# Activation transposes of a fused attention and feed-forward backward: from TensorE to DMA transposes

## Chip, cores and metric

One core of one Trainium2 chip. The metric is the device time of one execution in microseconds (us), median of the runs. The kernel is called "before", the changed one "after".

## The reference, cut to what matters

A pre-norm block with linear attention (32 heads of 20), then a SwiGLU feed-forward, and the gradients of everything. S = 2048 tokens, D = 640, F = 1728, all bf16.

```python
def _fwd_reference(A_x, A_wqkv, A_wo, B_x, B_w_gate, B_w_up, B_w_down):
    ...                               # _A_ref: linear attention, _B_ref: SwiGLU
    x = A_x
    h = x + _A_ref(_layernorm(x, axis=-1), A_wqkv, A_wo)
    h2 = h + _B_ref(_layernorm(h, axis=-1), B_w_gate, B_w_up, B_w_down)
    return h2

def reference(A_x, A_wqkv, A_wo, B_w_gate, B_w_up, B_w_down, B_x, grad_out):
    ...
    _out, _vjp = jax.vjp(_f, A_x, A_wqkv, A_wo, B_w_gate, B_w_up, B_w_down)
    return (_out, *_vjp(grad_out))    # output and six gradients
```

Forward products sum over features, weight gradients over tokens. In this kernel's matmuls the index that is summed over lies on the partitions (the 128 rows of a tile), so many activations are needed in both layouts: token-major ("tm", tokens on the partitions) and feature-major ("fm").

## The kernel before: the parts concerned

A transpose of a 128x128 block is a TensorE instruction into PSUM, up to eight of them side by side, and a copy out by VectorE or ScalarE in turn:

```python
def transpose_into(dst_fn, src_fn, nblk, rows_in, ps_pool, tag="tr", cols_in=P, group=8, eng=None):
    ...
    while b < nblk:
        nb = min(group, nblk - b)
        pt = ps_pool.tile([P, 8 * P], BF16, name="pt_" + tag, tag=tag)
        for j in range(nb):
            nc.tensor.transpose(out=pt[:cols_in, j * rows_in:(j + 1) * rows_in], in_=src_fn(b + j),
                                identity=ident[:rows_in, :rows_in])
        evac_copy(dst_fn(b, nb), pt[:cols_in, :nb * rows_in], eng)
        b += nb
```

The feed-forward loop takes two rows of 128 features ("a group") per pass: projections into feature-major rows, stores of the rows to DRAM for later stages, transposes of the rows into token-major strips, then weight gradients from the strips.

```python
strips = pb2.enter_context(tc.tile_pool(name="strips", bufs=1))
...
for grp in groups:                                   # 7 groups of 2 rows
    ...
    for i in grp:
        ...                                          # pg, pu, pdm matmuls; mT_row, dgT_row, duT_row
        nc.gpsimd.dma_start(out=scr_mT_v[:, i, :], in_=mT_row[:, :])
        nc.gpsimd.dma_start(out=scr_dgT_v[:, i, :], in_=dgT_row[:, :])
        nc.gpsimd.dma_start(out=scr_duT_v[:, i, :], in_=duT_row[:, :])
        for (row, strip) in ((mT_row, m_strip), (dgT_row, dg_strip), (duT_row, du_strip)):
            transpose_into(...)                      # 16 blocks each
        coff += fs
    ...                                              # acc: m_strip x dh2; accw: hn x dg_strip, du_strip
```

Later, in the backward attention, six tensors are transposed one after another, two of them after a reload from DRAM:

```python
pq_tm = ...; fm_to_tm(pq_tm, pqTr, D, psTD)
dnum_tm = ...; fm_to_tm(dnum_tm, dnumT, D, psTD)
...                                                  # dKV matmuls
nc.sync.dma_start(out=pk_tmr[:], in_=scr_pk_tm_v)
pkT = ...; tm_to_fm(pkT, pk_tmr, D, psTD)
nc.sync.dma_start(out=v_tmr[:], in_=scr_v_tm_v)
vT = ...; tm_to_fm(vT, v_tmr, D, psTD)
...                                                  # ps_dv and ps_dk matmuls need all of pkT and vT
```

## Time and profile before

| | before |
|---|---|
| median time | 1115.46 us (2 runs, 1115.44 to 1115.48) |
| TensorE busy | 1056.7 us, 95% of the span |
| transposes concerned | 1632 blocks of 128x128, about 93 us of TensorE issue |
| DMA | 134 MB, 120 GB/s over the span |
| feed-forward loop | 60.2 us a group, seven groups |

Read the busy shares first, to see which engine is full; then the chain that ended last, to see whether that engine also sets the end; then single groups. The prediction shows these lines.

### The profile page before, as it was taken

The page shows a single profiled execution, that of the slowest core. Times are in us where ns is not written, and L with a number is a line of the kernel's source. Part 1 is how long each engine was busy: PE and PEld are TensorE (multiplying, and loading weights), DVE is VectorE, ACT ScalarE, POOL GpSimd, SP SyncE. Part 2 cuts the span into 40 slices and gives each one's busy share as a digit, 9 for nine tenths or more (in the row PEclk, how much of TensorE's full clock was granted, in tenths as well). Part 3 has the DMA queues.
Part 4 walks back from the last instruction along what each step waited for, and adds up shares of the span by engine and source line. Part 5 has one row for each costly group of instructions (what it writes and reads, how often), then busy time and mean ns, then how long its engine had stood idle before and what let it go on. Part 6 is the DMA issues. An engine that isn't in the chain of part 4 may idle for free.

```text
span 1114.9 us, 20384 instructions
## 1 busy us (share of the span) xinstructions
PE 1056.7 (95%) x8337; PEld 714.7 (64%) x8337; DVE 571.8 (51%) x1441; ACT 483.0 (43%) x951; POOL 133.4 (12%) x224
## 2 busy tenths in 40 slices
PE   5899998999999999999996999599989999899998
PEld 2477665575847576666756777377767467577775
DVE  8766676727273545545361232234343985477321
ACT  5755587526262535345351010122233686744231
POOL 2100000120202111111312013000000000011110
PEclk9899899999999999999999999799999999999999
DMA  8244364312222222212045954955440039411110
GB/s 318 75 138 150 159 247 146 125 61 86 92 82 96 78 103 78 98 41 107 31 159 182 219 136 139 298 119 122 100 153 31 1 123 351 181 39 43 42 36 30
DMA packets 134669, 134.24 MB, mean 120 GB/s; under 512 B 92384, under 2 KB 115680, under 8 KB 134320
## 3 DMA queue, kind: packets, MB, share of 16 engines
q0 software_dynamic: 20208, 77.58, 18.8%
q1 hardware_dynamic: 85440, 48.03, 15.4%
q10 hardware_dynamic: 28928, 7.34, 3.4%
q8 instruction: 65, 1.06, 0.4%
q14 instruction: 28, 0.23, 0.1%
HBM read 71.50 MB, written 61.42 MB: 119 GB/s over the span
## 4 chain that ended last, share of the span: by engine, by line
PE 69%; DMA 6%; DVE 6%; issue 1%; ACT 1%; POOL 0%; POOLq 0%; DVEq 0%; ACTq 0%; SPq 0%
PE accw L561 10%; PE acch L663 10%; PE acc_dxn L837 6%; PE accf L621 6%; PE acc_dwqkv L856 6%; PE pu L498 4%; PE pg L494 4%; PE acc L552 4%; PE pt_trs L127 4%; PE pt_tr L127 3%; PE pdm L502 3%; DMA dgcols<-scr_dgT 3%; PE acc_dwo L697 2%; PE ps_do L721 2%; DVE dm L519 1%
## 5 line engine op out<-in xcount | busy, mean ns | idle before, releaser
L561 PEld LDWEIGHTS <-hn_tm 128*128 128x128 bf16 x1120 | 107.1, 98 | 16.0 <-issue 4.8
L494 PE MATMUL pg<-hnT,wg_blk 128*128 128x512 bf16 (+1 forms) x280 | 76.2, 384 | 3.3 <-DMA wg_blk<-in_B_w_gate_dram 3.3
L663 PE MATMUL acch<-wgT,dgcols 128*128 128x320 bf16 x448 | 67.9, 304 | 12.0 <-DMA dgcols<-scr_dgT 11.5
L498 PE MATMUL pu<-hnT,wu_blk 128*128 128x512 bf16 (+1 forms) x280 | 74.7, 379 | 0.0
L89 DVE CAST dw_sb<-accw 128x256 bf16<-128x256 f32 (+1 forms) x35 | 14.5, 415 | 111.7 <-PE accw L561 86.8
L502 PE MATMUL pdm<-dh2T,wdT 128*128 128x512 bf16 (+1 forms) x280 | 69.6, 379 | 1.1 <-ACT dm L511 1.0
L552 PE MATMUL acc<-dh_tm,m_strip 128*128 128x320 bf16 (+1 forms) x448 | 69.3, 299 | 0.0
L621 PE MATMUL accf<-wd_big,mcols 128*128 128x320 bf16 x448 | 64.8, 306 | 3.6 <-DMA mcols<-scr_mT 3.6
L663 PE MATMUL acch<-wuT,ducols 128*128 128x320 bf16 x448 | 66.4, 300 | 0.0
L856 PE MATMUL acc_dwqkv<-cur_tm,xn_tmr 128*128 128x320 bf16 x480 | 65.7, 299 | 0.0
L663 PEld LDWEIGHTS <-dgcols 128*128 128x128 bf16 x448 | 44.4, 99 | 30.4 <-DMA dgcols<-scr_dgT 11.8
L561 PE MATMUL accw<-dg_strip,hn_tm 128*128 128x256 bf16 (+1 forms) x560 | 60.5, 269 | 3.4 <-ACT dw_sb L91 2.9
L561 PE MATMUL accw<-du_strip,hn_tm 128*128 128x256 bf16 (+1 forms) x560 | 60.3, 269 | 0.7 <-DVE dw_sb L89 0.7
L856 PEld LDWEIGHTS <-xn_tmr 128*128 128x128 bf16 x480 | 46.9, 98 | 18.1
L621 PEld LDWEIGHTS <-mcols 128*128 128x128 bf16 x448 | 44.0, 100 | 22.1 <-DMA mcols<-scr_mT 3.7
L91 ACT CAST dw_sb<-accw 128x256 bf16<-128x256 f32 (+1 forms) x35 | 12.8, 364 | 103.8 <-PE accw L561 98.9
L214 ACT ACTIVATE lb_dy<-acch 128x320 bf16<-128x320 f32 x32 | 14.0, 436 | 97.6 <-PE acch L663 97.6
L663 PEld LDWEIGHTS <-ducols 128*128 128x128 bf16 x448 | 44.0, 98 | 17.3
L552 PEld LDWEIGHTS <-m_strip 128*128 128x128 bf16 (+1 forms) x448 | 41.8, 99 | 13.5 <-issue 0.3
L229 DVE SCALAR_TENSOR_TENSOR lb_t<-lb_dy,lb_nm,lb_t 128x640 bf16<-128x640 bf16 x32 | 28.2, 880 | 41.1 <-ACT lb_t L227 41.1
L502 PEld LDWEIGHTS <-wdT 128*128 128x128 bf16 (+1 forms) x280 | 27.0, 98 | 34.4 <-DVE wdT L89 3.1
L565 POOL DMA_DIRECT2D out_dram<-dw_sb x70 | 37.7, 539 | 79.5 <-DVE dw_sb L89 44.9
(264 smaller groups left out, 2068.2 us busy)
## 6 DMA issues: line engine op xcount, KB each, us to landing
scr_mT<-mT_row POOLq DMA_DIRECT2D x14, 512.0 KB, 2.9
scr_duT<-duT_row POOLq DMA_DIRECT2D x14, 512.0 KB, 3.7
scr_dgT<-dgT_row POOLq DMA_DIRECT2D x14, 512.0 KB, 2.9
ducols<-scr_duT ACTq DMA_DIRECT2D x16, 448.0 KB, 4.7
mcols<-scr_mT SPq DMA_DIRECT2D x16, 448.0 KB, 4.1
dgcols<-scr_dgT SPq DMA_DIRECT2D x16, 448.0 KB, 4.2
out_dram<-dw_sb POOLq DMA_DIRECT2D x60, 64.0 KB, 1.8
x_tm<-in_A_x_dram SPq DMA_DIRECT2D x4, 640.0 KB, 6.3
```

Of the source, the lines that this page charges most:

```text
L127: nc.tensor.transpose(out=pt[:cols_in, j * rows_in:(j + 1) * rows_in], in_=src, identity=ident[:rows_in, :rows_in])
L229: nc.vector.scalar_tensor_tensor(out=t2[:], in0=dy[:], scalar=nm[:, 0:1], in1=t1[:], op0=ALU.subtract, op1=ALU.subtract)
L494: nc.tensor.matmul(pg[:fs, :], lhsT=wg_blk[:, kt, coff:coff + fs], rhs=hnT[:, kt, cs], start=(kt == 0), stop=(kt == DT - 1))
L498: nc.tensor.matmul(pu[:fs, :], lhsT=wu_blk[:, kt, coff:coff + fs], rhs=hnT[:, kt, cs], start=(kt == 0), stop=(kt == DT - 1))
L502: nc.tensor.matmul(pdm[:fs, :], lhsT=wdT_i[:, kt, :], rhs=dh2T[:, kt, cs], start=(kt == 0), stop=(kt == DT - 1))
L552: nc.tensor.matmul(acc[:fs, :w], lhsT=m_strip[:, t, coff:coff + fs], rhs=dh2_tm[:, t, n0:n1], start=(t == 0), stop=(t == ST - 1))
L561: nc.tensor.matmul(acc[:, :gw], lhsT=hn_tm[:, t, dt_ * P:(dt_ + 1) * P], rhs=strip[:, t, :gw], start=(t == 0), stop=(t == ST - 1))
L565: nc.gpsimd.dma_start(out=o_ap[dt_ * P:(dt_ + 1) * P, gcol0:gcol0 + gw], in_=dw_sb[:, :gw])
L621: nc.tensor.matmul(acc[:, :w], lhsT=mcols[:, j, :], rhs=wd_nat[:, j, n0:n1], start=(j == 0), stop=(j == FT - 1))
L663: nc.tensor.matmul(acc[:, :w], lhsT=cols[:, j, :], rhs=wT[:, j, n0:n1], start=(k == 0), stop=(k == 2 * FT - 1))
L837: nc.tensor.matmul(acc[:, :w], lhsT=srcT[:, jj, t * P:(t + 1) * P], rhs=wqkvT[:, j, n0:n1], start=(k == 0), stop=(k == D3T - 1))
L856: nc.tensor.matmul(acc[:, :w], lhsT=xn_tmr[:, t, dt_ * P:(dt_ + 1) * P], rhs=cur_tm[:, t, n0:n1], start=(t == 0), stop=(t == ST - 1))
```

## The change

The intent is to free TensorE: it is the bound, and the DMA engines are mostly idle (busy share 0.38 over the span of before). All transposes of activations become DMA transposes on the SyncE queue, one per token tile ([128, 640], 5 blocks) or per feature tile ([128, 2048], 16 blocks). The small weight transposes stay on TensorE.

```diff
     def tm_to_fm(dstT, src_tm, W, ps_pool, eng=None, tag="tr"):
-        WT = W // P
-        for j in range(WT):
-            transpose_into(...)
+        for t in range(ST):
+            nc.sync.dma_start_transpose(out=dstT[:, :, t * P:(t + 1) * P], in_=src_tm[:, t, :])

     def fm_to_tm(dst_tm, srcT, W, ps_pool, eng=None, tag="tr"):
-        WT = W // P
-        for t in range(ST):
-            transpose_into(...)
+        for j in range(W // P):
+            nc.sync.dma_start_transpose(out=dst_tm[:, :, j * P:(j + 1) * P], in_=srcT[:, j, :])
 ...
     def tm_to_fm_tiles(dstT, src_tm, W, t0, nt, ps_pool, eng=None, tag="tr"):
-        ...
+        for t in range(t0, t0 + nt):
+            nc.sync.dma_start_transpose(out=dstT[:, :, t * P:(t + 1) * P], in_=src_tm[:, t, :])
 ...
                     for (row, strip) in ((mT_row, m_strip), (dgT_row, dg_strip), (duT_row, du_strip)):
-                        transpose_into(...)
+                        nc.sync.dma_start_transpose(out=strip[:, :, coff:coff + fs], in_=row[:fs, :])
```

More of the change, by code (lines that the diff above doesn't have):

```diff
@@ L132, in tm_to_fm @@
     def tm_to_fm(dstT, src_tm, W, ps_pool, eng=None, tag="tr"):
-        WT = W // P
-        for j in range(WT):
-            transpose_into(
-                dst_fn=lambda b0, nb, j=j: dstT[:, j, b0 * P:(b0 + nb) * P],
-                src_fn=lambda b, j=j: src_tm[:, b, j * P:(j + 1) * P],
-                nblk=ST, rows_in=P, ps_pool=ps_pool, eng=eng, tag=tag)
-    def fm_to_tm(dst_tm, srcT, W, ps_pool, eng=None, tag="tr"):
-        WT = W // P
-        for t in range(ST):
-            transpose_into(
-                dst_fn=lambda b0, nb, t=t: dst_tm[:, t, b0 * P:(b0 + nb) * P],
-                src_fn=lambda b, t=t: srcT[:, b, t * P:(t + 1) * P],
-                nblk=WT, rows_in=P, ps_pool=ps_pool, eng=eng, tag=tag)
+        for t in range(ST):
+            nc.sync.dma_start_transpose(out=dstT[:, :, t * P:(t + 1) * P], in_=src_tm[:, t, :])
+    def fm_to_tm(dst_tm, srcT, W, ps_pool, eng=None, tag="tr"):
+        for j in range(W // P):
+            nc.sync.dma_start_transpose(out=dst_tm[:, :, j * P:(j + 1) * P], in_=srcT[:, j, :])
     def layernorm_tiles(src_tm, dst_tm, mean, rstd, t0, nt, work, mode="bn"):
@@ L201, in tm_to_fm_tiles @@
     def tm_to_fm_tiles(dstT, src_tm, W, t0, nt, ps_pool, eng=None, tag="tr"):
-        WT = W // P
-        for j in range(WT):
-            transpose_into(
-                dst_fn=lambda b0, nb, j=j: dstT[:, j, (t0 + b0) * P:(t0 + b0 + nb) * P],
-                src_fn=lambda b, j=j: src_tm[:, t0 + b, j * P:(j + 1) * P],
-                nblk=nt, rows_in=P, ps_pool=ps_pool, eng=eng, tag=tag)
+        for t in range(t0, t0 + nt):
+            nc.sync.dma_start_transpose(out=dstT[:, :, t * P:(t + 1) * P], in_=src_tm[:, t, :])
     def ln_bwd_tile(acc_chunks, xhat_t, rstd_col, resid_t, dst_t, work):
@@ L527 @@
                     for (row, strip) in ((mT_row, m_strip), (dgT_row, dg_strip), (duT_row, du_strip)):
-                        transpose_into(
-                            dst_fn=lambda b0, nb, strip=strip, coff=coff, fs=fs: strip[:, b0:b0 + nb, coff:coff + fs],
-                            src_fn=lambda b, row=row, fs=fs: row[:fs, b * P:(b + 1) * P],
-                            nblk=ST, rows_in=fs, ps_pool=ps_tr, tag="trs", cols_in=P)
+                        nc.sync.dma_start_transpose(out=strip[:, :, coff:coff + fs], in_=row[:fs, :])
                     coff += fs
```

## The prediction

The sum was 0 (before the loop) + 10 (loop) + 8 (attention output) + 96 (four tensors) + 14 (last stage) = +128 us on 1115, rounded to 1240.

> **What bounds the kernel now.** I read the header of the page first, then the chain of work that ended last, then the groups of the transposes, then the windows by stage, and last the DMA queues, because the change moves work from TensorE to them.
>
> ```profile
> PE 1056.7 (95%) x8337; PEld 714.7 (64%) x8337; DVE 571.8 (51%) x1441; ACT 483.0 (43%) x951; POOL 133.4 (12%) x224
> PE 69%; DMA 6%; DVE 6%; issue 1%; ACT 1%; POOL 0%; POOLq 0%; DVEq 0%; ACTq 0%; SPq 0%
> ```
>
> TensorE is busy 95% of the span and carries 69% of the chain. There is hardly a stage where it waits: it is the bound nearly everywhere. So a microsecond of matmul issue taken away is worth about a microsecond, as long as nothing new makes TensorE wait. What the transposes cost it is in the groups by line and tile:
>
> ```profile
> L127 PE MATMUL pt_trs<-ident,mT_row 128*128 128x128 bf16 (+1 forms) x224 | 19.0, 217 | 1.2 <-DVE m_strip L89 0.3
> L127 PE MATMUL pt_trs<-ident,dgT_row 128*128 128x128 bf16 (+1 forms) x224 | 16.9, 217 | 0.2
> L127 PE MATMUL pt_trs<-ident,duT_row 128*128 128x128 bf16 (+1 forms) x224 | 16.6, 216 | 0.2
> ...
> L127 PE MATMUL pt_tr<-ident,dh_tm 128*128 128x128 bf16 x160 | 11.2, 219 | 0.5
> ```
>
> Busy time (the figure after the first bar) overlaps with neighbours; 217 ns is the latency of one, and they issue much faster. The chain in order of time has the pure rate in the backward attention stage:
>
> ```profile
> 910.04 8.63 PE pt_tr L127 x140
> ...
> 928.67 4.47 PE pt_tr L127 x80
> ...
> 933.57 4.64 PE pt_tr L127 x80
> ```
>
> 80 transposes take 4.5 to 4.6 us, 57 ns each, and there they stand on the chain with matmuls right before and behind. The windows say how much room the DMA engines have (columns: stretch, length, busy time of PE, PEld, DVE, ACT, POOL, granted clock, DMA share, GB/s):
>
> ```profile
> 305.00:366.00 61.00, 60.61 (x460) 39.97 (x459) 31.14 (x72) 26.52 (x46) 9.68 (x18) 1.00 0.24 86
> ...
> 908.00:930.00 22.00, 21.85 (x351) 21.21 (x350) 12.78 (x32) 11.84 (x20) 0.86 (x1) 1.00 0.94 335
> 930.00:961.00 31.00, 30.82 (x246) 17.73 (x244) 19.51 (x48) 29.98 (x48) 0.00 (x0) 1.00 0.52 189
> ```
>
> One group of the feed-forward loop (61 us, seven of them) leaves 76% of DMA free; the stage at 908 us, where four more tensors are to be transposed by DMA, has 94% busy already with reloads from DRAM.
>
> ```profile
> q1 hardware_dynamic: 85440, 48.03, 15.4%
> q10 hardware_dynamic: 28928, 7.34, 3.4%
> ```
>
> (Columns: packets, MB, share of 16 engines.) The second queue moves rows of 256 B: 3.4% of 16 engines' 1114.9 us is 606 us, over 28928 packets 21 ns each. 16 engines at 256 B in 21 ns are 195 GB/s; the first queue gives 32 ns a packet.
>
> [...]For DMA no row here shows a transpose. [...]All hangs on this rate.
>
> **The change part by part.** It removes 3x224 transposes of the feed-forward rows, and those of twelve tensors of 80 blocks each: 960. Together 1632 at 57 ns: 93 us of TensorE. In the loop there are 96 per group; the group's matmuls, at the rates of the chain, are 120 of 512 columns at 0.216 us (25.9), 64 of 320 at 0.136 (8.7) and 160 of 256 at 0.109 (17.5), 52.1 us against a period of 60.2. The ten small weight transposes stay (0.6 us), so 7.5 us per group, 52 us in seven, are what the loop can gain[...]. The evacuation copies go too: 41 us of ScalarE and 28 us of VectorE for the strips, but neither engine bounds this loop (26.5 and 31.1 of 61 us), so they are worth nothing.
>
> It adds 42 DMA transposes of [128, 2048] (16 blocks, 512 KB), 30 of the same size for the feature-to-token tensors, and 96 of [128, 640] (5 blocks, 160 KB): about 53 MB on top of 134 MB, all on the SyncE queue, which issues in order and also carries the weight loads and reloads.
>
> [...]To each I add 2 us from issue to landing, as the smallest stores of this trace need (1.8 to 2.1 us).
>
> Stage 1 (to 187 us): the transposes of the input follow LayerNorm[...]; those of the output gradient come off TensorE, 5 us; the second LayerNorm loses about what it gains. Sum 0.
>
> Loop: [...]the second row's three strips can only start when that row is done, about 3 us after its last matmul, behind the rest of the first row's. [...]TensorE has only 8.7 us of matmuls on the first strips before it needs the gradient strips; each strip tile has one buffer, so the next group's can't run ahead either. About 8 to 10 us of new wait per group against 7.5 gained: +1.5 times 7, +10.
>
> Backward attention: the attention output's transposes, pipelined by column block[...], +8 with the ones behind them. From 892 us, when buffers come free, four tensors in a row: [...]the kernel now starts the next matmuls at 938: +96. This is the biggest term: TensorE has only some 27 us of other work meanwhile.
>
> Last stage: [...]the first hidden behind 65 us of matmuls, the next two each behind 21.7[...], 8.4 us of TensorE transposes saved: +14.
>
> Sum 0+10+8+96+14 = +128: **1240 us**.
>
> **The rivals.** First, the transposes run near copy speed[...]. Then the loop gains 30 to 50 us, the four-tensor stage costs 0 to 30, the end gains 8: 1040 to 1085 us. For it: the 195 GB/s of the 256 B queue[...]. Against: [...]from 908 us the engines have 6% free. Second, [...]the loop[...] becomes DMA-bound (+25 times 7), the four-tensor stage +230, the rest some +150: about 1670 us[...]. Third, the rate is good but order costs: SyncE holds a load behind a transpose that waits for its source, and TensorE waits for a weight or a column block; some us per group, 20 to 60 us in all. It would make even the first rival a draw. Granted clock is no part of it: it is 0.9 to 1.0 now.
>
> **Range and chances.** [...]The draw is a narrow band of rates, one in seven. The slow side is open: 1240 with a range from 1070[...] to 1680[...]. Faster 0.17, within 2% 0.14, slower 0.69.
>
> **What would show it.** In the changed profile, the time from issue to landing and the spacing of the strip transposes give the rate[...]. TensorE's busy time should fall by some 90 to 120 us, to about 945, and its share to under 80%; its idle time should be put to DMA, largest before the matmuls that read the four backward tensors and before the gradient-strip matmuls of the loop. If the loop's period is under 56 us the rate is better than I think; if over 75 the loop is DMA-bound. If waits fall on weight loads instead, it is the order of the SyncE queue. I am wrong if the four tensors land within 60 us of each other, or if they are transposed earlier because buffers are free sooner than 892 us.

## The result, and the profile after

After: 1209.66 us median (1207.21 and 1212.12); the ratio to before is 1.0836, 95% interval 1.0773 to 1.0899. So it is slower. A ratio here is the mean time of one kernel's fast runs over that of the other's of the same rounds, so not quite the ratio of the medians.

The header and the chain of the page after:

```profile
PE 973.6 (81%) x6705; PEld 634.7 (53%) x6705; DVE 503.2 (42%) x1306; ACT 385.3 (32%) x813; POOL 134.2 (11%) x225
q1 hardware_dynamic: 296640, 100.74, 42.2%
PE 67%; DMA 18%; SPq 7%; DVE 3%; ACT 3%; issue 1%; POOLq 0%; DVEq 0%; ACTq 0%
```

TensorE did lose 83 us of busy time, as intended. But the chain has 18% of DMA instead of 6%, and a new member: 7% for SPq, the sequencer of SyncE, which before had none. The SyncE queue's packets went from 85440 to 296640.

Where the 90 us between the two profiled spans lie, from the first and last starts of a stage's matmuls in both traces:

| stretch (up to) | before | after | difference |
|---|---|---|---|
| first matmul of the feed-forward loop (pg) | 181.4 | 177.5 | -3.9 |
| first matmul of the next stage (accf): the loop | 431.4 | 467.8 | +36.4 |
| last matmul of acch | 207.4 | 208.3 | +0.9 |
| last matmul of ps_do | 68.6 | 78.6 | +10.0 |
| first matmul of acc_dxn: middle of the backward attention | 81.9 | 135.6 | +53.7 |
| first matmul of acc_dwqkv | 65.2 | 66.6 | +1.4 |
| end | 79.0 | 70.8 | -8.2 |

**The loop.** The chain of after in order of time (start, us, what), around the end of the first group:

```profile
208.32 14.52 DMA m_strip<-mT_row
...
222.88 6.87 PE acc L537 x32
229.76 2.29 PE accw L546 x21
```

The last projection of the group ends at 207 us. The transpose of the second row's first strip is issued at 208.3 and lands 14.5 us later. TensorE has the first row's matmuls on that strip until 211.3, and then stands for 11.6 us. The timeline of after says what was issued at that time (start, us; L512 to L514 are the row stores; other lines of VectorE, ScalarE and TensorE are left out):

```profile
206.82 4.51 PE L537 MATMUL acc<-dh_tm,m_strip 128*128 128x320 bf16 x32
207.64 0.53 POOL L512 DMA_DIRECT2D scr_mT<-mT_row  x1 [9.73 <-DVE mT_row L502]
207.75 0.47 SPq L458 DMA_DIRECT2D wu_blk<-in_B_w_up_dram  x1
208.32 7.42 SPq L516 DMA_TRANSPOSE m_strip<-mT_row  x1
208.36 0.53 POOL L514 DMA_DIRECT2D scr_duT<-duT_row  x1 [0.18 <-issue]
...
210.61 0.53 POOL L513 DMA_DIRECT2D scr_dgT<-dgT_row  x1 [1.72 <-DVE dgT_row L511]
```

In the same 3 us as the strip that TensorE waits for, three stores of the same rows (512 KB each, and nobody needs them for 400 us) start on the GpSimd queue; two weight loads of 320 KB (`wg_blk` and `wu_blk`) were issued just before. The windows of after (columns as in the prediction) for this wait, and for the rest of that group:

```profile
205.90:223.00 17.10, 5.54 (x39) 3.55 (x37) 4.04 (x10) 1.63 (x4) 2.14 (x4) 0.74 1.15 224
223.00:247.50 24.50, 24.50 (x198) 20.03 (x198) 2.61 (x6) 2.11 (x6) 5.39 (x10) 0.90 0.25 63
```

DMA engines full (share 1.15) and TensorE idle for most of it, then TensorE full and the DMA engines at a quarter. The granted clock is 0.74 in the wait and 0.90 after it, where the loop before had 1.00. The first 32 matmuls after the wait take 6.87 us in the chain. In the same trace, the 32 of the same shape just before the wait took 4.51. Over the seven groups, the groups by line of after put 71.7 us of idle TensorE on this one wait:

```profile
L537 PE MATMUL acc<-dh_tm,m_strip 128*128 128x320 bf16 (+1 forms) x448 | 75.1, 335 | 71.7 <-DMA m_strip<-mT_row 71.7
```

And the whole loop in the windows, before and after:

```profile
181.40:612.90 431.50, 420.18 (x3199) 276.04 (x3200) 217.09 (x505) 187.00 (x324) 72.79 (x130) 0.99 0.28 99
177.50:645.40 467.90, 384.22 (x2515) 245.94 (x2516) 191.25 (x459) 148.47 (x278) 73.54 (x131) 0.91 0.61 137
```

TensorE's idle time in the loop grew by 72 us (from 11 to 84), and its busy time fell by 36: that is the +36.

**The middle of the backward attention.** SyncE's timeline of after, and the load of v in that of before:

```profile
948.63 21.52 SPq L138 DMA_TRANSPOSE dnum_tm<-dnumT  x5
970.32 0.91 SPq L769 DMA_DIRECT2D pk_tmr<-scr_pk_tm  x1
982.05 21.02 SPq L134 DMA_TRANSPOSE pkT<-pk_tmr  x16
1003.18 0.51 SPq L773 DMA_DIRECT2D v_tmr<-scr_v_tm  x1
1013.50 21.04 SPq L134 DMA_TRANSPOSE vT<-v_tmr  x16
```

```profile
918.76 0.36 SPq L788 DMA_DIRECT2D v_tmr<-scr_v_tm  x1
```

A load, its 16 transposes, the next load, its 16 transposes: nothing overlaps. The load of v is issued only at 1003.2, when the sequencer is through with the transposes of pk; before, it was issued 10 us after the first transpose of this stage began (918.8 us against 908.6). And 16 transposes keep the sequencer busy for 21.0 us, one every 1.31 us. That is 160 KB in 1.31 us, 125 GB/s, with the DMA engines under 60% busy in this stretch (0.59 and 0.58).

**Theory.** (1) In the loop, latency: the second row's strips share the DMA engines with row stores that are in no hurry. (2) In the middle, the issue on SyncE: each transpose costs a minimum whatever its size, and reloads wait behind transposes in the queue's order. **Rival:** the bytes. A DMA transpose moves its bytes at some rate, all transposes together are too many, and neither order nor number of instructions matters.

### The profile page after: what moved, and what is told of

Read it like the earlier page. It is cut to its first block, busy times and chain, and to the rows that moved or that the text cites. A ratio compares the mean times of both kernels' runs of the same rounds, so it can differ in the third digit from the quotient of the medians.

```text
span 1205.2 us, 17218 instructions
## 1 busy us (share of the span) xinstructions
PE 973.6 (81%) x6705; PEld 634.7 (53%) x6705; DVE 503.2 (42%) x1306; ACT 385.3 (32%) x813; POOL 134.2 (11%) x225
## 4 chain that ended last, share of the span: by engine, by line
PE 67%; DMA 18%; SPq 7%; DVE 3%; ACT 3%; issue 1%; POOLq 0%; DVEq 0%; ACTq 0%
PE accw L546 10%; PE acch L648 9%; DMA m_strip<-mT_row 8%; PE acc_dxn L822 6%; PE acc_dwqkv L841 5%; PE pg L482 5%; PE pu L486 5%; PE pdm L490 5%; SPq L134 5%; PE accf L606 5%; PE acc L537 3%; DMA dgcols<-scr_dgT 2%; SPq L138 2%; PE ps_v L329 2%; PE ps_k L324 2%
## 5 line engine op out<-in xcount | busy, mean ns | idle before, releaser
L537 PE MATMUL acc<-dh_tm,m_strip 128*128 128x320 bf16 (+1 forms) x448 | 75.1, 335 | 71.7 <-DMA m_strip<-mT_row 71.7
L537 PEld LDWEIGHTS <-m_strip 128*128 128x128 bf16 (+1 forms) x448 | 48.6, 110 | 98.2 <-DMA m_strip<-mT_row 73.9
L482 PE MATMUL pg<-hnT,wg_blk 128*128 128x512 bf16 (+1 forms) x280 | 70.6, 383 | 6.1 <-issue 6.1
L486 PE MATMUL pu<-hnT,wu_blk 128*128 128x512 bf16 (+1 forms) x280 | 70.9, 384 | 0.0
L606 PE MATMUL accf<-wd_big,mcols 128*128 128x320 bf16 x448 | 65.2, 307 | 3.1 <-DMA mcols<-scr_mT 3.1
L546 PE MATMUL accw<-dg_strip,hn_tm 128*128 128x256 bf16 (+1 forms) x560 | 60.2, 269 | 1.0 <-DMA dg_strip<-dgT_row 1.0
L648 PEld LDWEIGHTS <-dgcols 128*128 128x128 bf16 x448 | 44.4, 99 | 30.2 <-DMA dgcols<-scr_dgT 11.6
L89 DVE CAST dw_sb<-accw 128x256 bf16<-128x256 f32 (+1 forms) x35 | 14.5, 415 | 107.8 <-PE accw L546 101.4
L89 DVE CAST dwd_sb<-acc 128x320 bf16<-128x320 f32 (+1 forms) x14 | 6.8, 486 | 116.4 <-PE acc L537 116.4
L793 PE MATMUL ps_dk<-vT,dKVbdT 128*128 128x512 bf16 x52 | 16.8, 429 | 40.7 <-DMA vT<-v_tmr 40.7
L91 ACT CAST dwd_sb<-acc 128x320 bf16<-128x320 f32 (+1 forms) x14 | 6.0, 426 | 129.2 <-PE acc L537 129.2
```

What stands on the lines that cost most here:

```text
L482: nc.tensor.matmul(pg[:fs, :], lhsT=wg_blk[:, kt, coff:coff + fs], rhs=hnT[:, kt, cs], start=(kt == 0), stop=(kt == DT - 1))
L486: nc.tensor.matmul(pu[:fs, :], lhsT=wu_blk[:, kt, coff:coff + fs], rhs=hnT[:, kt, cs], start=(kt == 0), stop=(kt == DT - 1))
L537: nc.tensor.matmul(acc[:fs, :w], lhsT=m_strip[:, t, coff:coff + fs], rhs=dh2_tm[:, t, n0:n1], start=(t == 0), stop=(t == ST - 1))
L546: nc.tensor.matmul(acc[:, :gw], lhsT=hn_tm[:, t, dt_ * P:(dt_ + 1) * P], rhs=strip[:, t, :gw], start=(t == 0), stop=(t == ST - 1))
L606: nc.tensor.matmul(acc[:, :w], lhsT=mcols[:, j, :], rhs=wd_nat[:, j, n0:n1], start=(j == 0), stop=(j == FT - 1))
L648: nc.tensor.matmul(acc[:, :w], lhsT=cols[:, j, :], rhs=wT[:, j, n0:n1], start=(k == 0), stop=(k == 2 * FT - 1))
```

## The experiments

All kernels gave correct results.

### Strips only

Before, with the last hunk of the change alone.

> Only the 42 strip transposes of the feed-forward loop go by DMA; the twelve other tensors stay on TensorE. From the two traces the loop (start of its first matmul to the first matmul of the next stage) grew from 425 to 468 us, so if the parts add up: about 1115 + 43 = 1158 us. Rival, that the loop is only slow because the SyncE queue also carries the other tensors: under 1125 us.

Measured 1152.34 us, ratio 1.0338. The wait on the first strip is there as in after (76.8 us of TensorE in seven waits). So the loop's loss does not need the other tensors on the queue. (The expectation took the loop of before as 425 us; it is 431 by the table above, and the sum then gives 1151.)

### Tensors only

After, with the strips back on TensorE (the last hunk undone).

> Only the twelve tensors go by DMA, the strips stay on TensorE. If the parts add up: 1115 + 94 - 43, about 1163 us, with about -10 us before the loop, +65 in the backward attention up to the matmuls of dk and dv, -8 in the last stage. Rival, that the two parts hurt each other through the shared queue: well under 1150 us.

Measured 1169.33 us, ratio 1.0477. The excesses of the two parts, 3.4% and 4.8%, make 8.2% together, against 8.4% for the whole change: the parts add, and hardly disturb each other.

### Rates alone

Before, with transposes appended that nobody reads:

```diff
+            for r in range(6):
+                t_big = mt.tile([P, ST, P], BF16, name=f"t_big{r}")
+                nc.sync.dma_start_transpose(out=t_big[:, :, :], in_=dvT[:, r % DT, :])
+            for r in range(16):   # t_mid: [P, DT, P] <- cur_tm[:, r, :]
+            ...
+            for r in range(16):   # t_one: [P, P] <- cur_tm[:, r, 0:P]
```

> The kernel before, with DMA transposes added at its end that nobody reads: 6 of [128, 2048], 16 of [128, 640], 16 of [128, 128], each into its own buffer, with little other traffic. Theory of a fixed issue cost: spacing of the [128, 640] ones 1.3 us as in the changed kernel, of the [128, 128] ones about 0.9 to 1.0, of the [128, 2048] ones 2.2 to 3 us. Rival, cost by bytes alone: 0.8 us and 0.16 us for the two smaller. The time of this kernel says nothing.

SyncE's timeline of this kernel, and the windows over the same stretches (TensorE does nothing; the last two columns are DMA share and GB/s):

```profile
1113.41 14.67 SPq L865 DMA_TRANSPOSE t_big<-dvT  x6
1128.12 21.29 SPq L868 DMA_TRANSPOSE t_mid<-cur_tm  x16
1149.45 20.55 SPq L871 DMA_TRANSPOSE t_one<-cur_tm  x16
```

```profile
1113.40:1128.10 14.70, 0.00 (x0) 0.00 (x0) 0.00 (x0) 0.00 (x0) 0.00 (x0) 0.52 1.03 192
1128.10:1149.40 21.30, 0.00 (x0) 0.00 (x0) 0.00 (x0) 0.00 (x0) 0.00 (x0) 0.50 0.66 131
1149.40:1170.00 20.60, 0.00 (x0) 0.00 (x0) 0.00 (x0) 0.00 (x0) 0.00 (x0) 0.50 0.16 32
```

Divided by the counts: one block costs 1.28 us, five blocks 1.33, sixteen 2.45. So there is a floor of about 1.28 us per instruction, and five blocks cost hardly more; I had expected the single block cheaper (0.9 to 1.0). Only the 16-block ones fill the DMA engines (1.03), at 512 KB in 2.45 us, 214 GB/s (the 192 of the window leaves out what lands after its end). The smaller ones leave the engines idle for a third of the time and more (0.66 and 0.16), while SyncE issues without a gap, so the floor is in the issue, not in the engines' rate. The rival of bytes falls for the [128, 640] form. What inside the issue takes the 1.28 us, no run shows.

### Stores behind

After, with the row stores on the SyncE queue, behind the transposes:

```diff
-                    nc.gpsimd.dma_start(out=scr_mT_v[:, i, :], in_=mT_row[:, :])
-                    ...                                     # dgT, duT
                     for (row, strip) in (...):
                         nc.sync.dma_start_transpose(out=strip[:, :, coff:coff + fs], in_=row[:fs, :])
+                    nc.sync.dma_start(out=scr_mT_v[:, i, :], in_=mT_row[:, :])
+                    ...                                     # dgT, duT
```

> The changed kernel, with the three stores of each feed-forward row to DRAM taken from the GpSimd queue and issued on the SyncE queue behind that row's transposes. Same bytes. Theory, that the wait of about 10 us a group is the second row's first strip sharing the DMA engines with those stores: its landing falls from 9 to 14 us to about 5, the loop's period from 66 to about 57, total about 1150 us. Rival, that the transposes' own rate sets it: landing and total as before within 1%, 1200 to 1215 us.

Measured 1143.30 us, the median of the three fast runs (1140.72 to 1147.77), ratio 1.0253; a fourth run was slow (1163.20) and is in neither. The same bytes give back 66 us of the 94, more than the loop's whole excess of 36. So the loop should now be better than before; in the mixed kernel below, which has the same loop, it takes 408.7 us against 431.4, and the group from 240.6 to 298.2 us takes 57.6 against 60.2. Since its profile is of a slow run, I take the landing times from the mixed kernel too (median us from issue to landing at the end of each line), and after's for comparison:

```profile
m_strip<-mT_row SPq DMA_TRANSPOSE x14, 9.2
du_strip<-duT_row SPq DMA_TRANSPOSE x14, 9.2
dg_strip<-dgT_row SPq DMA_TRANSPOSE x14, 4.4
```

```profile
m_strip<-mT_row SPq DMA_TRANSPOSE x14, 4.8
du_strip<-duT_row SPq DMA_TRANSPOSE x14, 5.3
dg_strip<-dgT_row SPq DMA_TRANSPOSE x14, 5.0
```

From 9.2 to 4.8 for the first strip, which is what it takes alone (4.8 us, median, in "rates alone"). So theory (1) holds: the stores made the strip late. The edit changed two things at once, the order and the queue of these stores (GpSimd to SyncE); no run separates them.

### Reloads on the GpSimd queue

```diff
-        nc.sync.dma_start(out=pk_tmr[:], in_=scr_pk_tm_v)
+        nc.gpsimd.dma_start(out=pk_tmr[:], in_=scr_pk_tm_v)
...                                                        # v_tmr likewise
```

> The changed kernel, with the reloads of two tensors (pk and v, token-major) issued on the GpSimd queue instead of SyncE, so that they don't stand behind transposes in SyncE's order. Theory of order: the stretch from 950 to 1036 us, where now load, 16 transposes, load, 16 transposes follow one another, loses the two loads (11.7 and 10.2 us): total about 1190. Rival, that the loads wait for buffers, not for the queue: no change within 1% (1200 to 1215).

Measured 1194.95 us, ratio 1.0691: 15 us less than after, three quarters of what was expected. The chain of its profile has the transposes of v following those of pk without a gap (1001.48, then 1002.87), where after had 10.2 us of load between; so it was the queue's order and not a buffer. Some of the other load's gain is lost again: of the first seven transposes of pk, one takes 4.66 us to issue and another 2.93, against 1.28 of the later ones. What slows them was not shown.

### Fewer, larger transposes

Four DMAs of [128, 2560] instead of 16 of [128, 640], for dh1, pk and v. The three results are now kept by token tile, and the matmuls read them with a stride:

```diff
-        pkT = bigD.tile(BIGSHAPE_FM, BF16, name="pkT", tag="B")
+        pkT = bigD.tile([P, ST, DT, P], BF16, name="pkT", tag="B")
...
-        for t in range(ST):
-            nc.sync.dma_start_transpose(out=dstT[:, :, t * P:(t + 1) * P], in_=src_tm[:, t, :])
+        for t in range(0, ST, 4):
+            nc.sync.dma_start_transpose(out=dstT[:, t:t + 4, :, :].rearrange("p t j r -> p (t j) r"),
+                                        in_=src_tm[:, t:t + 4, :].rearrange("p t d -> p (t d)"))
...
-                    nc.tensor.matmul(ps[:], lhsT=..., rhs=pkT[:, i, cs], ...)
+                    nc.tensor.matmul(ps[:], lhsT=..., rhs=pkT[:, 4 * sc:4 * sc + 4, i, :], ...)
```

> The changed kernel, with the token-to-feature transposes of three tensors of the backward attention (dh1, pk, v) issued as 4 DMAs of [128, 2560] each instead of 16 of [128, 640]; the transposed tensors get a layout by token tile, same bytes. From the run of the rates alone, an instruction costs 1.28 us at least and 2.45 us for 16 blocks: 4 x 3.1 = 12 us instead of 21 a tensor, so about 27 us less in all: 1182. Rival, cost by bytes: no change.

Measured 1181.05 us, ratio 1.0546: 29 us less than after for the same bytes, as the floor per instruction says. In its trace the four DMAs of v are issued 3.1 us apart, about 12.5 us in all, where the 16 took 21.0.

### All repairs

The three edits above together.

> The changed kernel with the three repairs at once: stores behind the strips, reloads of pk and v on the GpSimd queue, 4 larger DMAs instead of 16 for dh1, pk and v. Everything still by DMA. The gains measured one by one were 64, 15 and 29 us; if they add: 1210 - 108, about 1102 us, within 2% of the kernel before. Rival, that the second and third repair the same wait: about 1117 or more.

Measured 1118.01 us, ratio 1.0021 (0.9999 to 1.0043): level with before, and 16 us short of the expected sum (which counted 64 us for the stores; it is 66). That is the rival's number; what was in the way is another matter. By stages, the loop now gains 22 us on before, but from the last ps_do to the first acc_dxn it still loses 30 (112 against 82). The windows of its profile over the wait for dnum and over the transposes of pk and v:

```profile
882.00:909.00 27.00, 9.67 (x88) 8.51 (x86) 3.36 (x11) 1.76 (x3) 2.34 (x3) 0.62 1.08 297
909.00:942.00 33.00, 10.91 (x96) 6.36 (x93) 2.36 (x8) 2.83 (x5) 0.90 (x1) 0.64 1.08 223
```

The DMA engines are now full (1.08) for 60 us while TensorE works 20.6 of them. With order and issue repaired, by these shares the bytes bind here: the rival theory of the bytes fits what is left in this stage, four tensors and two reloads that come at one moment.

### Mixed

Each transpose where it seemed cheaper: strips by DMA with stores behind; x, dh2 and the second LayerNorm's output (before the loop) and dq, dk, dv (last stage) by DMA; the six of the backward attention's middle on TensorE again.

> Each transpose where the runs so far say it is cheaper: strips by DMA with the stores behind them, the three tensors before the loop and the three of the last stage by DMA, the six of the backward attention's middle on TensorE as in the kernel before. If parts add: 1115 - 10 (before the loop) - 15 (loop) - 8 (last stage) = about 1082 us. Rival, that DMA transposes before the loop gain nothing once measured alone: above 1095.

Measured 1087.23 us, ratio 0.9724 (0.9706 to 0.9741): faster than both kernels. By stages of its profile the loop gains 22.7 us and the end 9, while the start gains only 0.7: what the rival said of the transposes before the loop held, though not its total.

### One row late

The mixed kernel, with the loop reordered so that no strip is waited for: one row per pass, two buffers per strip, the weight gradients of a row after the projections of the next.

```diff
-    GRP = 2
+    GRP = 1
...
-            strips = pb2.enter_context(tc.tile_pool(name="strips", bufs=1))
+            strips = pb2.enter_context(tc.tile_pool(name="strips", bufs=2))
...
+                def weight_grads(grp=grp, ..., du_strip=du_strip):
+                    ...                                    # acc, accw and their stores, unchanged
+                if pending is not None:
+                    pending()
+                pending = weight_grads
```

> As the mixed kernel, but the feed-forward loop takes one row of 128 features at a time, has two buffers for each strip, and does a row's weight-gradient matmuls after the next row's projections, so that no strip is waited for. Theory, that latency of the second row's strips is all that the loop still loses: TensorE gapless there, 26.4 us a row, loop and total some 35 us less than the mixed kernel: about 1047. Rival, that the DMA engines are full (rate): no gain over the mixed kernel.

Measured 1168.55 us, ratio 1.0443: a plain miss, 81 us slower than the mixed kernel. The groups by line of its profile tell where:

```profile
L89 DVE CAST dw_sb<-accw 128x128 bf16<-128x128 f32 (+1 forms) x70 | 20.0, 285 | 204.0 <-DMA out_dram<-dw_sb 176.3
L91 ACT CAST dw_sb<-accw 128x128 bf16<-128x128 f32 (+1 forms) x70 | 18.3, 261 | 192.5 <-DMA out_dram<-dw_sb 174.1
```

The strips were no longer waited for, but the evacuations of the weight gradients were: each needs one of two small output buffers, whose store to DRAM now runs at the time of the strips and row stores (in one pass the strips are issued from 307.6 us and the row stores from 316.1, and the evacuations at 317 to 324 us had waited 4.3 to 6.7 us for a store to land). TensorE in turn waited 75.2 us for these evacuations, in 29 waits.

### One row late, deeper output buffers

```diff
-    dw_sb = dwo.tile([P, gwa], BF16, name="dw_sb")
+    dw_sb = dwo.tile([P, gwa], BF16, name="dw_sb", bufs=10)
```

> The late-by-one-row kernel, which lost 81 us to the mixed one, with ten instead of two buffers for the small weight-gradient tiles before they are stored. Its trace put the loss to evacuations that wait for those stores (350 us of waits of VectorE and ScalarE in all). Theory, that these stores queue behind strips and row stores on the shared DMA engines and only their two buffers hold TensorE back: total about 1050 to 1075. Rival, that twice as many, half as wide stores and matmuls are the loss: above 1130.

Measured 1052.39 us, ratio 0.9432 (0.9414 to 0.9450). One pass of its loop in the windows:

```profile
261.05:287.56 26.51, 26.40 (x257) 18.23 (x258) 14.07 (x37) 10.74 (x22) 5.95 (x11) 1.00 0.65 157
```

TensorE is full at clock 1.00, with the DMA engines at 0.65 under it. A row takes 26.5 us, two rows 53.0 against the 60.2 of a group before: nearly all of the 7.5 us that the prediction counted. The stores of the small tiles do take longer now (4.9 us at the median), but nobody waits. This is the fastest kernel.

### No strips, no middle

Only the tensors before the loop and of the last stage by DMA.

> Only the three tensors before the loop and the three of the last stage go by DMA; the strips and the six of the backward attention's middle stay on TensorE. From the stage times of the two traces: 1115 - 10 - 8 = about 1097. Then the mixed kernel's 1087 owes 10 us to its loop. Rival, that these stages gain nothing: 1115.

Measured 1108.38 us, ratio 0.9933 (0.9899 to 0.9967), within 2% of before: 7.5 us gained where 18 were expected. By stages of its profile the end gains 8.6 us as thought, but the start only 1.7, and the acc_dxn stage loses 2.8. Before that stage, TensorE waits for a weight reload; in before the transposes of dq stood in this wait and cost nothing (2.7 us of idle time left). Now it idles through it (9.7 us), and the slowest acc_dxn matmuls take 471 ns where in before none took over 300. So moving work off the bound engine gains nothing where it filled a wait. The mixed kernel differs from this one in the strips and their stores alone, which are thus worth 21 us there.

### One row late, strips on TensorE

The fastest kernel with only its strip transposes put back on TensorE.

> The fastest kernel so far (late by one row, deeper output buffers, 1052 us), with only the strips' transposes put back on TensorE. If it is the DMA transposes that win there, and not the new order of the loop: the loop's 672 transposes cost TensorE about 52 us again, total about 1100 us. Rival, that the new order alone brings the gain: below 1070.

Measured 1096.10 us, ratio 0.9809 (0.9772 to 0.9845). So the order of the loop alone does not do it: moving the strips to DMA is worth 44 us there, of the 52 that the prediction worked out for them as the most. The order, with its buffers and the stores behind, is worth something by itself: this kernel has its strips on TensorE as "no strips, no middle" has (1108.38), and is 12 us faster.

## Why the prediction came out, point by point

The direction and the time were right (1240 forecast, 1209.66 measured, inside a wide range of 1070 to 1680). But the sum owes that to luck, to errors that partly cancelled: for its terms 0+10+8+96+14 the traces show -4, +36, about +11, +54 and -7 (the last is +1.4 and -8.2).

- **What is removed: right in kind, a little less than forecast.** TensorE's busy time fell by 83 us (forecast 90 to 120), its share to 81% (forecast under 80%). "One row late, strips on TensorE" shows that 44 of the loop's 52 us are to be had.
- **The rate, one for every form: mis-sized, and wrong in form.** The figure that I took was my estimate, shown by no trace. Measured, it is not one rate: 1.28 us at least per instruction, 1.33 us for the 160 KB of a token tile (123 GB/s), 2.45 us for 512 KB alone (214 GB/s, with the DMA engines full at a share of 1.03; the other transfers of before moved 335 GB/s at 0.94, from 908 to 930 us). From issue to landing the same 512 KB take 4.8 us alone, and 9.2 (median) to 14.5 beside stores. A strip and a token tile alone are both faster than I took them to be.
- **The loop, +10: mis-sized, +36.** The step "About 8 to 10 us of new wait per group against 7.5 gained" named the right cause of a wait, the second row's strips, and its size is 10.2 us (71.7 over seven). The place was one step off: I put it before the gradient strips, and it stands before the second row's first strip (`m_strip`; for `dg_strip` TensorE waited 1.0 us in all). Three terms failed. I took the middle of my range instead of its upper end. "Granted clock is no part of it" is wrong: after each wait TensorE restarts slowly, 6.87 us for 32 matmuls instead of 4.51 in the first group, and 1.3 to 2.4 us more in each of the seven, 12 in all. And the transposes freed less than 52: busy time fell by 36, with these 12 that is 48. Together +72 of idle time, +12 and -48 are the +36. The granted clock is low in the same places: 0.50 to 0.52 where TensorE does nothing in "rates alone", 0.74 over the wait in the loop. In the mixed kernel gaps of 2.3 and 3.1 us were each followed by such a restart (6.19 us for the 32, where the 32 before the gap took 4.51); at which gap it begins, no run shows. I also did not see the cause of the wait: not the rate, but stores that share the engines. "Stores behind" shows it.
- **Four tensors, +96: mis-sized, +54.** The place and the wait were right. The four took 101 us from the first issue (934.9) to the last landing (1036), less than I had reckoned, because the rate was better (a token tile of pk or v every 1.31 us); and 22 of the 101 are the two reloads in series (11.7 and 10.2), for which I had counted much less. That is my third rival, the order of SyncE's queue; "reloads on the GpSimd queue" gave 15 us back.
- **The last stage, +14: wrong in sign, -7.** I had two tensors stick out, each from behind 21.7 us of matmuls. They took 16 us each to issue (1133.3 to 1149.0 and 1149.0 to about 1165), and were hidden. The step that failed is the rate again.
- **The rivals.** The first (near copy speed, 1040 to 1085) did not come about as the change was written. Its total was reached, 1052 us, but with the middle's six tensors back on TensorE and some 12 us from order and buffers alone. The second (much slower transposes, about 1670) is out for the change's own forms: five blocks took 1.33 us together and sixteen 2.45; only a single block by itself pays 1.28.

What stays open: what in the issue takes the 1.28 us, whether the order or the queue of the row stores delayed the strips, and whether the middle of the backward attention could be spread in time, by buffers freed earlier, so that DMA would win there too; it was not tried.

## What to carry to other kernels

A DMA transpose paid most here where its result was needed later (44 us in the loop with rows late, 21 where strips were still waited for a little): give it a double buffer and do other work between, make each one large (29 us less here for the same bytes), and put stores that nobody waits for behind it in the queue (66 us here). Where the result was needed at once, as with four tensors in a row, TensorE was the better place in these runs (82 us for that stretch in before, 112 by DMA with all repairs). And when a transfer starts to share the engines with others, look at every small output buffer near it: they may be the next wait, as two of them cost 116 us here.
